# First product of seven experts by Strassen's block products, on one core

## The chip, the cores and the metric

The kernel runs on one core of a Trainium2 chip. A core has a matrix engine (TensorE, in the profile PE, with its weight loads as PEld), three engines for elementwise work (VectorE or DVE, ScalarE or ACT, GpSimd or POOL), a synchronisation engine (SP) and DMA queues. Each engine works through its own queue of instructions in order. Matmuls write into PSUM, which has eight banks of 128 x 512 f32; DVE and ACT read them there, GpSimd works on SBUF alone. The metric is the device time of one launch in microseconds. Before the change it was 794.83 us, the median of three runs (791.57 to 795.60).

## The reference, cut to what matters

Two stages follow each other: an attention over sorted blocks, whose output is `x` with N = 3072 rows and D = 512 columns, and a mixture of eight experts with F = 1024 hidden columns.

```python
logits = x @ w_gate
P = np.exp(logits - logits.max())
for _ in range(8):                       # the gate
    P /= P.sum(1, keepdims=True) + 1e-09
    P /= P.sum(0, keepdims=True) + 1e-09
    P *= N / E
out = np.zeros((N, D))
for e in range(E):
    h = np.maximum(x @ w1[e], 0.0)       # first product
    out += P[:, e:e + 1] * (h @ w2[e])   # second product
```

The gate needs the logits of all rows, so it can begin only when the attention of all four batches is done.

## The kernel before, in words

The program is written with a tile framework that gives buffers and semaphores and fixes, when the program is built, the order in which each engine's queue holds its instructions. That order can differ from the order of the source lines; on the chip it doesn't change any more.

**Attention.** Four batches of 768 rows. Their output lands transposed in `xtT` (128 partitions x 4 blocks of D x 3072 rows, bf16), and `logits` (L241) writes `glog`. While batch `bb` is in the attention, expert 0 is computed for batch `bb - 1` (`expert0`, L302): the two generators take turns on TensorE. Expert 0 for the last batch is left for after the attention.

**Gate.** L340 to L381. An identity `I128`, which `make_identity` writes on GpSimd, is used by the first matmul (L358) to find the greatest logit; then eight rounds of four DVE operations, one matmul for the column sums (L377) and three DVE operations. Meanwhile TensorE works on expert 0's last batch (L383) and on expert 1. Then 24 DVE scalings (L386) multiply expert 0's part of the sum `osbl` (f32, all 3072 rows) by its gate.

**Experts 1 to 7.** For each expert, six chunks of 512 rows go through `expert` (L280). A chunk's first half is eight blocks of 128 hidden columns: four matmuls of 128 x 128 by 128 x 512 over D into one bank (L285), then a relu on ACT into `hTs` (L287). Its second half is four blocks of 128 rows: eight matmuls over the hidden columns into one bank (L292), then DVE adds the bank times the gate to `osbl` (L395). A chunk has 64 matmuls, an expert 384. For the last expert each finished block of rows goes out by DMA (L399).

**Weights.** `load_expert` (L77) loads `w1e` and `w2e` of one expert, 1 MB each in SBUF, from f32 in HBM; the DMAs are issued from GpSimd's queue. There are buffers for four experts, in the pools `wp` and `wp2`, and expert e + 2 is loaded when expert e begins.

Of the kernel before, what the change touches and what calls it, by code (L numbers as in the profile page):

```python
# [24 lines left out]
def kernel(  # L25
# [23 lines left out]
    mps = ctx.enter_context(tc.tile_pool(name="mps", bufs=2))  # L49
    actx = ExitStack()  # L50
    kvp = actx.enter_context(tc.tile_pool(name="kvp", bufs=2))
    perp = actx.enter_context(tc.tile_pool(name="perp", bufs=1))
    vsp = actx.enter_context(tc.tile_pool(name="vsp", bufs=1))
# [11 lines left out]
    def load_batch(bb, n):  # L65
        for d, name in ((vt, "vt"), (kt, "kt"), (qt, "qt")):
            d[bb] = kvp.tile([128, 8, 384], BF16, name=name, bufs=1 if d is vt else 2)
        for l0 in range(0, 8, n):
            for d, src in ((vt, v), (kt, k), (qt, q)):
                nc.gpsimd.dma_start(  # L70
                    out=d[bb][:, l0:l0 + n, :],
                    in_=src[bb, l0:l0 + n].rearrange("h (p kk) d -> p h (kk d)", kk=6))

    w1t = {}
    w2t = {}

    def load_expert(e, pool):  # L77
        w1t[e] = pool.tile([128, 4, F], BF16, name="w1e")
        w2t[e] = pool.tile([128, 8, Dm], BF16, name="w2e")
        nc.gpsimd.dma_start(out=w1t[e], in_=moe_w1[e].rearrange("(kk k) f -> k kk f", k=128))  # L80
        nc.gpsimd.dma_start(out=w2t[e], in_=moe_w2[e].rearrange("(fb k) f -> k fb f", k=128))

    Ibig = ones.tile([128, 128], BF16)
# [4 lines left out]
    load_expert(0, wp)  # L88
    load_batch(1, 4)


# [33 lines left out]
    xtT = xtp.tile([128, 4, N], BF16)  # L125
# [36 lines left out]
    def queries(bb, hp, bank, first):  # L162

        qps = bank([128, 6, 128], BF16)
        if first:
            for h in range(2):
                for kk in range(6):
                    nc.tensor.matmul(qps[64 * h:64 * h + 64, kk, :],  # L168
                                     qt[bb][:, 2 * hp + h, kk * 64:kk * 64 + 64],
                                     Ibig, is_transpose=True, start=True, stop=True)  # L170
        else:
            qr = sp.tile([128, 6, 2, 64], BF16, name="qr")
            nc.gpsimd.tensor_copy(  # L173
                qr.rearrange("p kk h d -> p h kk d"),
                qt[bb][:, 2 * hp:2 * hp + 2].rearrange("p h (kk d) -> p h kk d", d=64))
# [74 lines left out]
    def attention(bb, bank, first=False):  # L250
        if first:
            for hp in range(4):
                queries(bb, hp, bank, True)
            for l0 in (0, 4):
                yield from sort_values(bb, l0, 4, bank)
        else:
            yield from sort_values(bb, 0, 8, bank)
        for s in range(7):
            if s < 4:
                if not first:  # L260
                    queries(bb, s, bank, False)
# [18 lines left out]
    def expert(e, c0, n, hp, op, done):  # L280
        hTs = mps.tile([128, 8, 512], BF16, name="hTs")
        for fb in range(8):
            hps = hp.tile([128, 512], F32, name="hps")
            for kk in range(4):
                nc.tensor.matmul(hps[:, 0:n], w1t[e][:, kk, fb * 128:(fb + 1) * 128],  # L285
                                 xtT[:, kk, c0:c0 + n], start=(kk == 0), stop=(kk == 3))
            nc.scalar.activation(out=hTs[:, fb, 0:n], in_=hps[:, 0:n], func=AF.Relu)  # L287
            yield
        for tt in range(n // 128):
            oacc = op.tile([128, Dm], F32, name="oacc")  # L290
            for fb in range(8):
                nc.tensor.matmul(oacc, hTs[:, fb, tt * 128:(tt + 1) * 128],  # L292
                                 w2t[e][:, fb, :], start=(fb == 0), stop=(fb == 7))
# [5 lines left out]
    def keep(t, oacc):  # L299
        nc.vector.tensor_copy(osbl[:, t, :], oacc)  # L300

    def expert0(bb, hp, op):  # L302
        for c in range(2):
            yield from expert(0, bb * S + c * 384, 384, hp, op, keep)
# [15 lines left out]
    with ExitStack() as c2:  # L320
        pa = c2.enter_context(tc.tile_pool(name="pa", bufs=4, space=bass.MemoryType.PSUM,
                                           reuse_waits="tile"))
        hp1 = c2.enter_context(tc.tile_pool(name="hp1", bufs=2, space=bass.MemoryType.PSUM,
                                            reuse_waits="tile"))
        op1 = c2.enter_context(tc.tile_pool(name="op1", bufs=2, space=bass.MemoryType.PSUM,
                                            reuse_waits="tile"))
        bank1 = lambda shape, dt: pa.tile(shape, dt, name="bank", tag="bank")
        for bb in range(1, B):
            build_r(bb, nc.gpsimd, 4)
            if bb + 1 < B:  # L330
                load_batch(bb + 1, 8)
            else:
                load_expert(1, wp)
            work = [attention(bb, bank1), expert0(bb - 1, hp1, op1)]
            while work:
                work = [w for w in work if next(w, 0) is None]
    actx.close()


    wp2 = ctx.enter_context(tc.tile_pool(name="wp2", bufs=2))  # L340
    mpc = ctx.enter_context(tc.tile_pool(name="mpc", bufs=1))
    gp = ctx.enter_context(tc.tile_pool(name="gp", bufs=2, space=bass.MemoryType.PSUM,
                                        reuse_waits="tile"))
    hp = ctx.enter_context(tc.tile_pool(name="hp", bufs=3, space=bass.MemoryType.PSUM,
                                        reuse_waits="tile"))
    op = ctx.enter_context(tc.tile_pool(name="op", bufs=3, space=bass.MemoryType.PSUM,
                                        reuse_waits="tile"))
    load_expert(2, wp2)

    onesc = mpc.tile([128, 128], F32)  # L350
    nc.vector.memset(onesc, 1.0)
# [31 lines left out]
    for _ in expert0(B - 1, hp, op):  # L383
        pass
    for t in range(NT):
        nc.vector.tensor_scalar(out=osbl[:, t, :], in0=osbl[:, t, :],  # L386
                                scalar1=glog[:, t, 0:1], scalar2=None, op0=ALU.mult)


    for e in range(1, E):  # L390
        if e + 2 < E:
            load_expert(e + 2, wp2 if (e + 2) % 4 in (2, 3) else wp)

        def add(t, oacc):
            nc.vector.scalar_tensor_tensor(  # L395
                out=osbl[:, t, :], in0=oacc, scalar=glog[:, t, e:e + 1],
                in1=osbl[:, t, :], op0=ALU.mult, op1=ALU.add)
# [36 lines left out]
```

## Time and profile before

| what | value |
|---|---|
| median of three runs | 794.83 us |
| span of the profiled execution, first to last instruction | 792.7 us |
| TensorE busy | 748.6 us, 94% of the span |
| DVE, ACT, GpSimd busy | 235.4, 287.6, 45.4 us |
| mean granted TensorE clock | 0.970 |
| one whole expert, 302.8 to 385.7 us | 82.9 us |
| data moved by DMA | 39.45 MB |

The profile is of one execution. Its own time is known as the span; the launch's time holds a little more than the span. A row of the groups or of the timeline names the line of the kernel, the engine, the operation, the tile written and the tile read, the shapes and a count. The figure in brackets behind a row of the timeline is how long the engine stood idle before it, and what released it. Busy time of TensorE is modelled at the ends of matmuls, so stretches of many matmuls say more than the duration of one.

### The profile page before, as it was taken

To read this page: it belongs to the slowest core of one execution; us is meant where nothing else is said; L and a number is where in the kernel's file an instruction comes from. 1 tells how busy PE (TensorE), PEld (TensorE's weight loads), DVE (VectorE), ACT (ScalarE), POOL (GpSimd) and SP (SyncE) were. 2 spreads that over 40 slices of the span, in tenths; PEclk is the share of its full clock that TensorE was granted. 3 is DMA by queue.
4 is the path that set the end of the run, shared out by engine and by line. 5 is a ranking of instruction groups with operands and counts; after the bars stand their busy time and mean duration, and the time that the engine had idled before them with its cause. 6 is when DMAs were issued, how large, how long until landed. Compare 5 with 4: busy or idle time off the path is not lost.

```text
span 792.7 us, 10003 instructions
## 1 busy us (share of the span) xinstructions
PE 748.6 (94%) x4244; PEld 368.0 (46%) x4244; DVE 235.4 (30%) x502; ACT 287.6 (36%) x524; POOL 45.4 (6%) x61
## 2 busy tenths in 40 slices
PE   2497989999999999999999999999999999999997
PEld 1374646565444444444444444444444444444443
DVE  4233524464871212212121222212121221212122
ACT  3353454543224243332424233342423333242432
POOL 3341110001000000000000000000000000000000
PEclk9658998999999999999999999999999999999999
DMA  9998250209800051003300240000000000002212
GB/s 163 224 212 173 41 120 2 81 2 186 132 1 1 1 82 25 1 0 56 52 1 0 33 74 0 1 1 1 0 1 1 1 0 1 1 0 80 80 67 93
DMA packets 33836, 39.45 MB, mean 50 GB/s; under 512 B 1664, under 2 KB 25984, under 8 KB 33792
## 3 DMA queue, kind: packets, MB, share of 16 engines
q0 software_dynamic: 25648, 26.22, 21.0%
q1 hardware_dynamic: 8144, 12.59, 4.8%
q8 instruction: 33, 0.54, 0.3%
q14 instruction: 11, 0.09, 0.0%
HBM read 55.60 MB, written 9.44 MB: 82 GB/s over the span
## 4 chain that ended last, share of the span: by engine, by line
PE 86%; DMA 7%; DVE 4%; ACT 1%; issue 1%; POOL 1%; POOLq 0%; ACTq 0%
PE hps L285 40%; PE oacc L292 40%; DMA vd<-vs 3%; DMA vsb<-vd 3%; PE bank L222 2%; DMA qt<-in_q_dram 1%; PE bank L206 1%; DVE osbl L386 1%; PE bank L236 1%; ACT vs L149 1%; PE bank L190 1%; PE bank L147 0%; PE bank L177 0%; PE gps L377 0%; PE bank L246 0%
## 5 line engine op out<-in xcount | busy, mean ns | idle before, releaser
L287 ACT ACTIVATE hTs<-hps 128x512 bf16<-128x512 f32 (+1 forms) x400 | 232.8, 583 | 414.4 <-PE hps L285 414.3
L285 PE MATMUL hps<-xtT,w1e 128*128 128x512 bf16 (+1 forms) x1600 | 354.1, 375 | 0.0
L292 PE MATMUL oacc<-w2e,hTs 128*128 128x512 bf16 x1536 | 345.8, 379 | 0.4 <-DVE osbl L395 0.4
L395 DVE SCALAR_TENSOR_TENSOR osbl<-oacc,glog,osbl 128x512 f32<-128x512 f32 x168 | 125.9, 750 | 437.4 <-PE oacc L292 437.4
L285 PEld LDWEIGHTS <-w1e 128*128 128x128 bf16 x1600 | 156.1, 99 | 173.3 <-issue 4.6
L292 PEld LDWEIGHTS <-hTs 128*128 128x128 bf16 x1536 | 147.8, 98 | 173.3 <-issue 0.9
L212 ACT ACTIVATE atp<-bank 96x384 bf16<-96x384 f32 x64 | 27.7, 483 | 44.4 <-PE bank L222 29.8
L222 PE MATMUL bank<-vsb,atp 96*96 96x128 bf16 x256 | 23.8, 255 | 19.2 <-DMA vsb<-vd 19.2
L222 PEld LDWEIGHTS <-atp 96*96 96x96 bf16 x256 | 22.1, 152 | 24.1 <-DMA vsb<-vd 20.5
L195 DVE CAST kTs<-bank 128x384 bf16<-128x384 f32 x32 | 16.8, 578 | 33.4 <-PE bank L190 33.4
L229 DVE TENSOR_TENSOR og<-bank,recips 96x256 bf16<-96x256 f32 x64 | 24.2, 410 | 0.4
L300 DVE COPY osbl<-oacc 128x512 f32<-128x512 f32 x24 | 16.5, 688 | 21.9 <-PE oacc L292 21.5
L80 POOL DMA_DIRECT2D w1e<-in_moe_w_dram x8 | 6.2, 771 | 277.5 <-PE hps L285 246.7
L228 DVE RECIPROCAL recips<-bank 96x4 f32<-96x4 f32 x64 | 9.9, 170 | 37.3 <-PE bank L222 37.0
L206 PEld LDWEIGHTS <-kTs 64*96 64x96 bf16 x256 | 14.5, 130 | 10.3 <-issue 6.4
L149 ACT CAST vs<-bank 128x384 bf16<-128x384 f32 x32 | 13.8, 507 | 14.7 <-PE bank L147 12.6
L206 PE MATMUL bank<-qTs,kTs 64*96 64x96 bf16 x256 | 18.3, 219 | 0.3 <-ACT atp L212 0.2
L180 ACT COPY qTs<-bank 128x768 bf16<-128x768 bf16 x16 | 12.9, 818 | 5.8 <-PE bank L168 4.0
L173 POOL COPY qr<-qt 128x768 bf16<-128x768 bf16 x12 | 9.9, 833 | 58.6 <-PE bank L177 55.7
L312 PE MATMUL bank<-Ibig,Prep 32*128 32x32 bf16 x8 | 0.5, 188 | 12.7 <-DVE Prep L123 12.7
L236 PE MATMUL bank<-Ibig,og 96*128 96x96 bf16 x128 | 10.1, 225 | 1.2 <-DVE og L229 1.2
L236 PEld LDWEIGHTS <-og 96*128 96x128 bf16 x128 | 7.8, 108 | 4.1 <-DVE og L229 2.8
(65 smaller groups left out, 146.1 us busy)
## 6 DMA issues: line engine op xcount, KB each, us to landing
w1e<-in_moe_w_dram POOLq DMA_DIRECT2D x8, 1024.0 KB, 8.1
w2e<-in_moe_w_dram POOLq DMA_DIRECT2D x8, 1024.0 KB, 10.9
out_dram<-osbl SPq DMA_DIRECT2D x24, 256.0 KB, 2.0
vd<-vs SPq DMA_DIRECT2D x3, 768.0 KB, 9.2
vsb<-vd SPq DMA_DIRECT2D x3, 768.0 KB, 5.7
vt<-in_v_dram POOLq DMA_DIRECT2D x4, 384.0 KB, 9.0
kt<-in_k_dram POOLq DMA_DIRECT2D x4, 384.0 KB, 10.3
qt<-in_q_dram POOLq DMA_DIRECT2D x4, 384.0 KB, 12.0
```

Source lines behind the costliest of these rows:

```text
L149: nc.scalar.copy(vs[:, :, h, :], vps.rearrange("p (kk d) -> p kk d", d=64))
L195: nc.vector.tensor_copy(kT[bb, hp][:, :, :, 3 * b:3 * b + 3], kps.rearrange("p kk (i c) -> p i c kk", i=8))
L206: nc.tensor.matmul(sps[0:96, j, :], kT[bb, hp][r, i].rearrange("p c kk -> p (c kk)"), qT[bb, hp][r, 16 * i:16 * i + 16].rearrange("p c kk ...
L212: nc.scalar.activation(out=at[bb, hp, h, b][0:96], in_=sps[0:96], func=AF.Exp, scale=scale)
L222: nc.tensor.matmul(ops[0:96, j].rearrange("p a d -> p (a d)"), at[bb, hp, h, b][0:96, j, :], mkap(vsbt[bb % 2], [[VW, 96], [NB * 512 - a, ...
L229: nc.vector.tensor_mul(og[bb, hp][0:96, 4 * b:4 * b + 4, h, :], ops[0:96, :, 0, :], mkap(recips, [[recips.ap[0][0], 96], [1, 4], [0, 64]]))
L236: nc.tensor.matmul(xps[:, i, :], og[bb, hp][0:96, i].rearrange("p h d -> p (h d)"), Ibig[0:96, 0:96], is_transpose=True, start=True, stop= ...
L285: nc.tensor.matmul(hps[:, 0:n], w1t[e][:, kk, fb * 128:(fb + 1) * 128], xtT[:, kk, c0:c0 + n], start=(kk == 0), stop=(kk == 3))
L287: nc.scalar.activation(out=hTs[:, fb, 0:n], in_=hps[:, 0:n], func=AF.Relu)
L292: nc.tensor.matmul(oacc, hTs[:, fb, tt * 128:(tt + 1) * 128], w2t[e][:, fb, :], start=(fb == 0), stop=(fb == 7))
L300: nc.vector.tensor_copy(osbl[:, t, :], oacc)
L395: nc.vector.scalar_tensor_tensor(out=osbl[:, t, :], in0=oacc, scalar=glog[:, t, e:e + 1], in1=osbl[:, t, :], op0=ALU.mult, op1=ALU.add)
```

## The change

For experts 1 to 7 the first product is put together by a scheme of Strassen's with seven block products in place of eight. Rows are taken in three blocks of 1024. In a block, D is cut into two halves, the hidden columns into two halves of 512, and the rows into two halves of 512. So `w1` has the blocks a11, a21 (first half of D; first and second half of the hidden columns), a12, a22 (second half of D), `x` has b11, b12 (first half of D; first and second 512 rows), b21, b22, and the hidden part has c11, c12, c21, c22. A step of `hidden` computes 128 columns of each half for all 1024 rows. It forms seven products of two matmuls each in four banks:

- y = a11 (b12 - b22), kept in s3, then + (a11 + a12) b22, which gives c12;
- z = (a21 + a22) b11, kept in s2, then + a22 (b21 - b11), which gives c21;
- v = (a11 + a22)(b11 + b22), kept in s1, then + (a12 - a22)(b21 + b22);
- w = (a21 - a11)(b11 + b12);
- GpSimd makes s3 = s3 - s2 and s1 = s1 + s3; then c22 = w + s1, and c11 = v + (z + s3 - y), on DVE.

All four results go through a relu into `hT` (two buffers of 128 x 8 x 1024, bf16): c12 and c21 on ACT, c11 and c22 by a custom DVE instruction that adds two operands and clips the sum from below at 0. s1, s2, s3 and t are single f32 buffers.

The sums of blocks are made once and kept in bf16: `xc` (five of `x` for each of the three blocks of rows; block 0 on DVE, blocks 1 and 2 on GpSimd) ahead of the gate, and `wc` (ten instructions per expert, on GpSimd; two buffers). Expert 1's are ahead of the gate too, those of expert e + 1 are written into the loop over expert e.

The second product of a block of 1024 rows, `output`, runs while the next block's `hidden` runs; the two generators take turns, in steps. In block 0 of expert 1 there is no earlier block, and behind block 2 of expert 7 there is `output` alone. PSUM is used as six banks for `hidden` and two for `output`. The pool `wp2` goes: there are buffers for two experts, and expert e + 1 is loaded during expert e, `w1` at its beginning and `w2` behind its first block of rows.

```diff
-    def load_expert(e, pool):
-        w1t[e] = pool.tile([128, 4, F], BF16, name="w1e")
-        w2t[e] = pool.tile([128, 8, Dm], BF16, name="w2e")
+    def load_w1(e):
+        w1t[e] = wp.tile([128, 4, F], BF16, name="w1e")
         nc.gpsimd.dma_start(out=w1t[e], in_=moe_w1[e].rearrange("(kk k) f -> k kk f", k=128))
+
+    def load_w2(e):
+        w2t[e] = wp.tile([128, 8, Dm], BF16, name="w2e")
         nc.gpsimd.dma_start(out=w2t[e], in_=moe_w2[e].rearrange("(fb k) f -> k fb f", k=128))
...
-    wp2 = ctx.enter_context(tc.tile_pool(name="wp2", bufs=2))
     mpc = ctx.enter_context(tc.tile_pool(name="mpc", bufs=1))
+    xcp = ctx.enter_context(tc.tile_pool(name="xcp", bufs=1))
+    wcp = ctx.enter_context(tc.tile_pool(name="wcp", bufs=2))
+    htp = ctx.enter_context(tc.tile_pool(name="htp", bufs=2))
+    fsp = ctx.enter_context(tc.tile_pool(name="fsp", bufs=1))
...
-    load_expert(2, wp2)
+    xc = xcp.tile([128, 5, 2, N // 2], BF16)
+    wct = {}
+
+    def sum_x(p, eng):
+        ta, tb = (slice(1024 * p + 512 * i, 1024 * p + 512 * i + 512) for i in range(2))
+        b11, b12, b21, b22 = (xtT[:, k:k + 2, t] for k in (0, 2) for t in (ta, tb))
+        for j, (a, b, o) in enumerate(((b11, b22, ALU.add), (b12, b22, ALU.subtract),
+                                       (b21, b11, ALU.subtract), (b11, b12, ALU.add),
+                                       (b21, b22, ALU.add))):
+            eng.tensor_tensor(out=xc[:, j, :, 512 * p:512 * p + 512], in0=a, in1=b, op=o)
+
+    def sum_w(e):
+        wct[e] = wcp.tile([128, 5, 2, F // 2], BF16, name="wc")
+        for kk in range(2):
+            a11, a21 = (w1t[e][:, kk, f:f + 512] for f in (0, 512))
+            a12, a22 = (w1t[e][:, 2 + kk, f:f + 512] for f in (0, 512))
+            for j, (a, b, o) in enumerate(((a11, a22, ALU.add), (a21, a22, ALU.add),
+                                           (a11, a12, ALU.add), (a21, a11, ALU.subtract),
+                                           (a12, a22, ALU.subtract))):
+                nc.gpsimd.tensor_tensor(out=wct[e][:, j, kk, :], in0=a, in1=b, op=o)
+                yield
+
+    sum_x(0, nc.vector)
+    for _ in sum_w(1):
+        pass
+    sum_x(1, nc.gpsimd)
+    sum_x(2, nc.gpsimd)
 
     onesc = mpc.tile([128, 128], F32)
     nc.vector.memset(onesc, 1.0)
     I128 = mpc.tile([128, 128], F32)
     make_identity(nc, I128)
...
-    for e in range(1, E):
-        if e + 2 < E:
-            load_expert(e + 2, wp2 if (e + 2) % 4 in (2, 3) else wp)
...
-        for c in range(6):
-            for _ in expert(e, c * 512, 512, hp, op, add):
-                pass
...
+    bk = ctx.enter_context(tc.tile_pool(name="bk", bufs=6, space=bass.MemoryType.PSUM,
+                                        reuse_waits="tile"))
+    op = ctx.enter_context(tc.tile_pool(name="op2", bufs=2, space=bass.MemoryType.PSUM,
+                                        reuse_waits="tile"))
...
+    def hidden(e, p, i, hT):
...
+        def add(ps, wa, xa, first):
+            for kk in range(2):
+                nc.tensor.matmul(ps, wa[:, kk, :], xa[:, kk, :],
+                                 start=(first and kk == 0), stop=(kk == 1),
+                                 skip_group_check=True)
...
+        y = bank()
+        add(y, a11, xc[:, 1, :, xs], True)
+        s3 = wide("s3")
+        nc.scalar.copy(s3, y)
+        z = bank()
+        add(z, wc[:, 1, :, fs], b11, True)
+        s2 = wide("s2")
+        nc.scalar.copy(s2, z)
+        nc.gpsimd.tensor_tensor(out=s3, in0=s3, in1=s2, op=ALU.subtract)
+        yield
+        v = bank()
+        add(v, wc[:, 0, :, fs], xc[:, 0, :, xs], True)
+        s1 = wide("s1")
+        nc.scalar.copy(s1, v)
+        nc.gpsimd.tensor_tensor(out=s1, in0=s1, in1=s3, op=ALU.add)
+        add(y, wc[:, 2, :, fs], b22, False)
+        nc.scalar.activation(out=c12, in_=y, func=AF.Relu)
+        yield
+        w = bank()
+        add(w, wc[:, 3, :, fs], xc[:, 3, :, xs], True)
+        add(z, a22, xc[:, 2, :, xs], False)
+        nc.scalar.activation(out=c21, in_=z, func=AF.Relu)
+        nc.vector._custom_dve(TENSOR_ADD_SAT, out=c22, in0=w, in1=s1, s0=TOP, s1=0.0)
+        t = wide("t")
+        nc.vector.tensor_tensor(out=t, in0=z, in1=s3, op=ALU.add)
+        yield
+        add(v, wc[:, 4, :, fs], xc[:, 4, :, xs], False)
+        nc.vector.tensor_tensor(out=t, in0=t, in1=y, op=ALU.subtract)
+        nc.vector._custom_dve(TENSOR_ADD_SAT, out=c11, in0=v, in1=t, s0=TOP, s1=0.0)
+        yield
+
+    def output(e, p, i, hT):
+        for j in range(2):
+            tt = 4 * j + i
+            t = 8 * p + tt
+            oacc = op.tile([128, Dm], F32, name="oacc")
+            for fb in range(8):
+                nc.tensor.matmul(oacc, hT[:, fb, tt * 128:(tt + 1) * 128],
+                                 w2t[e][:, fb, :], start=(fb == 0), stop=(fb == 7))
+                if fb == 3:
+                    yield
...
+    last = None
+    for e in range(1, E):
+        if e + 1 < E:
+            load_w1(e + 1)
+            sums = sum_w(e + 1)
+        else:
+            sums = iter(())
+        for p in range(3):
+            hT = htp.tile([128, 8, 1024], BF16, name="hT")
+            for i in range(4):
+                work = [hidden(e, p, i, hT)]
+                if last:
+                    work.append(output(*last[0:2], i, last[2]))
+                while work:
+                    work = [w for w in work if next(w, 0) is None]
+                if p or i > 1:
+                    next(sums, 0)
+            if p == 0 and e + 1 < E:
+                load_w2(e + 1)
+            last = (e, p, hT)
+    for i in range(4):
+        for _ in output(*last[0:2], i, last[2]):
+            pass
```

More of the change, by code (lines that the diff above doesn't have):

```diff
@@ L9 @@
 from concourse import bass_utils, mybir
+from concourse.dve_ops import TENSOR_ADD_SAT
 from concourse.masks import make_identity
@@ L48 @@
     xtp = ctx.enter_context(tc.tile_pool(name="xtp", bufs=1))
-    mps = ctx.enter_context(tc.tile_pool(name="mps", bufs=2))
     actx = ExitStack()
+    mps = actx.enter_context(tc.tile_pool(name="mps", bufs=2))
     kvp = actx.enter_context(tc.tile_pool(name="kvp", bufs=2))
@@ L87 @@
     nc.gpsimd.dma_start(out=wg, in_=moe_w_gate.rearrange("(kk k) e -> k kk e", k=128))
-    load_expert(0, wp)
+    load_w1(0)
+    load_w2(0)
     load_batch(1, 4)
@@ L277, in attention, with expert @@
         yield
-    def expert(e, c0, n, hp, op, done):
-        hTs = mps.tile([128, 8, 512], BF16, name="hTs")
+    def expert(e, c0, n, hsb, hp, op, done):
+        hTs = hsb()
         for fb in range(8):
@@ L300, in keep, with expert0 @@
         nc.vector.tensor_copy(osbl[:, t, :], oacc)
-    def expert0(bb, hp, op):
+    def expert0(bb, hsb, hp, op):
         for c in range(2):
-            yield from expert(0, bb * S + c * 384, 384, hp, op, keep)
+            yield from expert(0, bb * S + c * 384, 384, hsb, hp, op, keep)
     with tc.tile_pool(name="ps0", bufs=8, space=bass.MemoryType.PSUM,
@@ L332 @@
             else:
-                load_expert(1, wp)
-            work = [attention(bb, bank1), expert0(bb - 1, hp1, op1)]
+                load_w1(1)
+                load_w2(1)
+            work = [attention(bb, bank1),
+                    expert0(bb - 1, lambda: mps.tile([128, 8, 384], BF16, name="hTs"), hp1, op1)]
             while work:
@@ L337 @@
     actx.close()
-    wp2 = ctx.enter_context(tc.tile_pool(name="wp2", bufs=2))
     mpc = ctx.enter_context(tc.tile_pool(name="mpc", bufs=1))
[L342 to L347, printed above, removed]
@@ L348 @@
-    load_expert(2, wp2)
+    xcp = ctx.enter_context(tc.tile_pool(name="xcp", bufs=1))
+    wcp = ctx.enter_context(tc.tile_pool(name="wcp", bufs=2))
+    htp = ctx.enter_context(tc.tile_pool(name="htp", bufs=2))
+    fsp = ctx.enter_context(tc.tile_pool(name="fsp", bufs=1))
+    gctx = ExitStack()
+    gp = gctx.enter_context(tc.tile_pool(name="gp", bufs=2, space=bass.MemoryType.PSUM,
+                                         reuse_waits="tile"))
+    hp = gctx.enter_context(tc.tile_pool(name="hp", bufs=3, space=bass.MemoryType.PSUM,
+                                         reuse_waits="tile"))
@@ new lines @@
+    op = gctx.enter_context(tc.tile_pool(name="op", bufs=3, space=bass.MemoryType.PSUM,
+                                         reuse_waits="tile"))
+    xc = xcp.tile([128, 5, 2, N // 2], BF16)
[7 more added lines that the diff above has]
+            eng.tensor_tensor(out=xc[:, j, :, 512 * p:512 * p + 512], in0=a, in1=b, op=o)
@@ L381 @@
         nc.vector.tensor_mul(glog, glog, mkap(cs1, [cs1.ap[0], [0, NT], cs1.ap[1]]))
-    for _ in expert0(B - 1, hp, op):
+    for _ in expert0(B - 1, lambda: htp.tile([128, 8, 1024], BF16, name="hT"), hp, op):
         pass
@@ L387 @@
                                 scalar1=glog[:, t, 0:1], scalar2=None, op0=ALU.mult)
-    for e in range(1, E):
-        if e + 2 < E:
-            load_expert(e + 2, wp2 if (e + 2) % 4 in (2, 3) else wp)
-        def add(t, oacc):
+    gctx.close()
+    bk = ctx.enter_context(tc.tile_pool(name="bk", bufs=6, space=bass.MemoryType.PSUM,
+                                        reuse_waits="tile"))
+    op = ctx.enter_context(tc.tile_pool(name="op2", bufs=2, space=bass.MemoryType.PSUM,
+                                        reuse_waits="tile"))
@@ new lines, with bank, wide @@
+    TOP = 3.0e38
+    def hidden(e, p, i, hT):
+        ta, tb = (slice(1024 * p + 512 * j, 1024 * p + 512 * j + 512) for j in range(2))
+        fs = slice(128 * i, 128 * i + 128)
+        xs = slice(512 * p, 512 * p + 512)
+        def add(ps, wa, xa, first):
[3 more added lines that the diff above has]
+                                 skip_group_check=True)
+        def bank():
+            return bk.tile([128, 512], F32, name="bk")
+        def wide(name):
+            return fsp.tile([128, 512], F32, name=name)
+        wc, w1 = wct[e], w1t[e]
+        a11, a22 = w1[:, 0:2, fs], w1[:, 2:4, 512 + 128 * i:640 + 128 * i]
+        b11, b22 = xtT[:, 0:2, ta], xtT[:, 2:4, tb]
+        c11, c12 = hT[:, i, 0:512], hT[:, i, 512:1024]
+        c21, c22 = hT[:, 4 + i, 0:512], hT[:, 4 + i, 512:1024]
+        y = bank()
[28 more added lines that the diff above has]
+        yield
@@ L399, in add @@
                 nc.sync.dma_start(out=out[t * 128:(t + 1) * 128, :], in_=osbl[:, t, :])
-        for c in range(6):
-            for _ in expert(e, c * 512, 512, hp, op, add):
-                pass
+            yield
+    last = None
[21 more added lines that the diff above has]
+            pass
 _INS = ['q', 'k', 'v', 'sort_net', 'moe_w_gate', 'moe_w1', 'moe_w2']
```

## The prediction

> **What bounds the kernel now.** I read the page's shares first, then the groups by line, then the table by stages, then the timeline around the gate (the routing weights `glog`), because the change works on both sides of it.
>
> The page's busy times, and three of its costliest groups (line, engine, op, tile, count, then busy us and mean ns):
>
> ```profile
> PE 748.6 (94%) x4244; PEld 368.0 (46%) x4244; DVE 235.4 (30%) x502; ACT 287.6 (36%) x524; POOL 45.4 (6%) x61
> ...
> L287 ACT ACTIVATE hTs<-hps 128x512 bf16<-128x512 f32 (+1 forms) x400 | 232.8, 583 | 414.4 <-PE hps L285 414.3
> ...
> L395 DVE SCALAR_TENSOR_TENSOR osbl<-oacc,glog,osbl 128x512 f32<-128x512 f32 x168 | 125.9, 750 | 437.4 <-PE oacc L292 437.4
> ...
> w1e<-in_moe_w_dram POOLq DMA_DIRECT2D x8, 1024.0 KB, 8.1
> ```
>
> TensorE is busy 94% of the span, and ACT and DVE wait for it (the last columns). The table by stages (stretch, length, then PE, PEld, DVE, ACT, POOL busy us, granted clock, DMA):
>
> ```profile
> 177.00:179.80 2.80, 1.91 (x39) 1.49 (x40) 2.34 (x9) 0.00 (x0) 2.15 (x4) 0.89 0.20 11
> 179.80:182.40 2.60, 2.60 (x16) 1.25 (x14) 0.56 (x2) 0.49 (x1) 1.54 (x3) 0.50 1.07 181
> ...
> 302.80:385.70 82.90, 82.90 (x386) 37.55 (x384) 18.01 (x24) 28.66 (x48) 1.64 (x2) 1.00 0.16 26
> ```
>
> One expert is 384 matmuls in 82.90 us with TensorE never idle at full clock: 0.2159 us each. All other engines have room. The row at 179.8 shows what a thin stretch costs: after 2.8 us in which TensorE was busy 1.91, it ran 2.6 us at clock 0.50.
>
> GpSimd's own timeline, where the change puts most of its sums (start, us, engine, line):
>
> ```profile
> 26.30 2.12 POOL L135 TENSOR_TENSOR R<-Pb,mask 128x512 bf16<-128x512 f32 x2
> ...
> 102.18 0.94 POOL L70 DMA_DIRECT2D vt<-in_v_dram  x1 [16.60 <-PE bank L147]
> 103.12 0.84 POOL L173 COPY qr<-qt 128x768 bf16<-128x768 bf16 x1
> ...
> 180.18 0.33 POOL masks.py:199 TENSOR_SCALAR_AFFINE_SELECT I<-I 128x128 f32<-128x128 f32 x1
> ```
>
> A two-input elementwise of 512 columns takes GpSimd 1.04 us (2.12 and, elsewhere, 2.06 for two), a one-input copy of 768 takes 0.83. The identity I128, which the gate needs first, is ready at 180.5.
>
> TensorE's timeline at the gate:
>
> ```profile
> 174.71 1.03 PE L292 MATMUL oacc<-w2e,hTs 128*128 128x512 bf16 x4
> ...
> 186.38 0.81 PE L292 MATMUL oacc<-w2e,hTs 128*128 128x512 bf16 x3
> 187.12 0.38 PE L358 MATMUL gps<-I,gm 128*1 128x128 f32 x2
> ...
> 205.55 0.38 PE L285 MATMUL hps<-xtT,w1e 128*128 128x512 bf16 x1
> ...
> 215.34 0.39 PE L377 MATMUL gps<-cs,onesc 128*128 128x8 f32 x2 [0.35 <-DVE cs L375]
> ```
>
> The gate's chain runs from L358 at 187.12 to its eighth column sum, which ends at 215.73: 28.6 us. It is hidden: TensorE works on experts 0 and 1 between its steps and starts expert 1 at 205.55. Check of this reading: 205.55 + 2688 x 0.2159 + 1.8 for the five gate matmuls after it + 4.1 from the last matmul to the end = 791.8, against a span of 792.7. The median of the runs shown, 794.83, lies 2.1 above that span; I add 2.1 at the end.
>
> **What the change saves.** A step (an expert's 128 columns of each half, 1024 rows) has 14 hidden matmuls in place of 16. There are 7 x 3 x 4 = 84 steps: 168 x 0.2159 = 36.3 us less TensorE work. A step with its 16 output matmuls is 30 x 0.2159 = 6.48 us.
>
> **Engines in a step.** ACT: three copies and two relus, 5 x 0.60 (L287 at 128x512 is 597 ns) = 3.0. DVE: two L395 sums, two tensor_tensor, two custom adds; none of the last four is in the trace, I take 0.75 each for those with two wide inputs (L395) and 0.70 for the custom (between L300's 0.69 and 0.75): 4.4. GpSimd: two adds, 2.1. All are below 6.48, and the single buffers s1, s2, s3, t close a loop of about 3.4 us (ACT 0.60 twice, GpSimd 1.05, DVE 0.75, hand-overs 0.4). The tightest place is v of the next step, which takes the bank of y: y is read last by t - y, at about 6.6 us of its step, and v is wanted at 8.2. So the plain step stays bound by TensorE, with 1.6 us to spare. These edits cost nothing while that margin holds.
>
> **Where GpSimd's queue breaks it: the gate.** The scheduler fixes each queue's order in the built program. After the attention GpSimd's queue reads:
>
> ```
> xc sums x2, wc sums of expert 1 x10, xc sums x8, I128 memset, I128 select,
> w1 load of expert 2, wc sums of expert 2 x2, w2 load, wc sums x8, then the s3 and s1 adds of expert 1
> ```
>
> I128 stands behind 20 sums. The first waits for the last L292 of expert 0's third batch (175.74), so it starts near 176.0. The xc sums have 1024 columns, of which the trace has none: I take 2 x 1.04 = 2.08. So 10 x 2.08 + 10 x 1.04 = 31.2, with memset and select (0.23 and 0.33 and gaps, 0.9) I128 is ready at 208.1. TensorE, in order, gets to its first gate matmul after 32 hidden and 14 output matmuls, at 186.4 + 3.0 = 189.4, and stands for 18.7 us. Behind it is the rest of expert 0, about 13 us of work, which no longer covers the chain: the last four column sums follow each other with nothing between. By the chain's old length TensorE is free at 208.1 + 28.6 = 236.7 and DVE at 237.5.
>
> DVE then has the 24 scalings of `osbl` by `glog` (L386: 9.59 us) queued ahead of its first work for expert 1, which starts at 247.1. Block 0 of expert 1 has no output matmuls to hide this. Its four steps go by the loop of 3.4 us: the first z + s3 ends at 248.55, t - y of step 2 at 256.1, then v, its copy and v again bring TensorE to block 1 at 258.0. Left to TensorE alone it would have been 236.7 + 12.1 = 248.8. DVE's five xc sums cost nothing: the maximum of `glog` behind them is not wanted until 208.
>
> **Where it breaks it again: once per expert.** At the start of experts 2 to 6 the queue reads: w1 load of the next expert, s3 add of step 0, one wc sum, s1 add of step 0, nine wc sums, s3 add of step 1. Count from the expert's first matmul. The load waits for the last use of the old w1, in the third quarter of the step before (-2.15), goes out at -1.9 and lands 8.1 later, at 6.2; the wc sum waits for it. Behind it: s1 add of step 0 at 7.3 to 8.3 (wanted at 3.1), nine sums to 17.7, s3 and s1 adds of step 1 to 19.8. DVE's add of w and s1 waits, and behind it, in order, z + s3 and t - y. t - y of step 0 ends at 10.5: v of step 1 waits from 8.2 to 10.6. t - y of step 1 ends at 22.1: v of step 2 starts at 22.2, where it would have been 14.7. That is 7.5 us an expert, in waits of 2.4 and 5.1; five times, 37.5. Expert 7 has no sums to make.
>
> **Clock.** A wait of 5.1 us without a matmul has no like in this stage of the trace; the row at 179.8 puts 2.6 us at half clock behind a much thinner gap, 1.3 us lost. Bounds: nothing, and the same behind both waits (2.6 an expert). I take 1.3 for the long one: 6.5.
>
> [...]
>
> **Sum.** 258.0, + the rest of TensorE's work, (2520 - 56) x 0.2159 = 532.0, + 37.5 + 6.5 + 4.1 = 838.1 of span; + 2.1: 840 us.
>
> The unknown that matters is GpSimd's price. From below: the copy's rate, 0.83 / 768 x 512 = 0.56 per sum, which would mean that a second input is free. From above: the longest row of L135, 1.11. I take 1.04, the same operation. The new custom add has L229's form (410 ns at 256) below and no upper row; it would have to reach 1.5 before the margin of 1.6 goes. The landing has 7.8 below and 16.7 above (one early load beside many others); I take 8.1, as nothing else loads then.
>
> [...]
>
> **The rivals.**
> 1. GpSimd's adds on bf16 cost far less than L135's, and both waits shrink. At 0.56: I128 at 193.7, block 1 at 242.2, 1.2 an expert, no clock loss: 242.2 + 532.0 + 6.0 + 4.1 + 2.1 = 786, the only road I see to faster. It decides below about 0.6 per sum. Against it: six rows of L135 from 1.04 to 1.11. At 0.83 the same sum gives 818, still slower.
> 2. The waits per expert are covered (the load lands early and the adds overtake): 840 - 44 = 796, no change. Against it: the order is fixed, and nine sums alone are 9.4 us against a margin of 1.6. If only the load were instant, the loss is 4.4 an expert: 824.
> 3. DVE becomes the bound: a custom add of 2.5 makes 8.0 a step, 84 x 1.5 = 126 more before what it hides: some 920. Nothing in the trace speaks for so slow an add.
>
> **How the numbers follow.** Main case 0.84, rival 1 0.05, rival 2 0.05, rival 3 and the like 0.06. The range goes from GpSimd at 0.83 (818, less 4 without clock loss) to GpSimd at 1.11 (+6), the clock lost behind both waits (+6.5) and landings 2 us later, a quarter of the way to 16.7 (+10): 814 to 862. About 0.5% is what can be told from no change here: rival 1 gives faster 0.04 and part of same, rival 2 the rest of same, 0.04; slower 0.92.
>
> **What would show it.** Hidden matmuls number 1176 plus 256. GpSimd's first two-input sums at about 1.04 and 2.08 us; TensorE idle near 189 to 208 on GpSimd's I128; a second pause until about 237; 24 scalings on DVE ahead of the first custom add; at the start of experts 2 to 6 two pauses of TensorE of 2 to 3 and about 5 us, released by DVE, with DVE waiting for GpSimd and GpSimd for a DMA; plain steps of 6.5 us. Wrong if the sums take half, if the order counts for less because landings come earlier, or if plain steps are longer than 6.5.

## The result and the profile after

The changed kernel takes 869.26 us (median of 4 runs, 868.27 to 869.63) against 793.39 us for the kernel before (4 runs, 791.57 to 795.6): a ratio of 1.0963, 95% interval 1.0941 to 1.0985. The profiled execution has a span of 867.6 us. The forecast was 840, with a range of 814 to 862: the direction was right, the loss is 29 us larger than forecast, and the time lies above the range.

The page of the changed kernel, busy times and three groups (line, engine, op, tile, count, then busy us and mean ns, then idle time and its releaser), and the weight load:

```profile
PE 735.5 (85%) x4011; PEld 356.5 (41%) x4076; DVE 473.9 (55%) x843; ACT 318.2 (37%) x608; POOL 359.5 (41%) x309
...
L466 POOL TENSOR_TENSOR s<-s,s 128x512 f32<-128x512 f32 x84 | 106.4, 1266 | 290.6 <-ACT s L465 273.0
...
L480 DVE CUSTOM_DVE_ANT_0 hT<-bk,s 128x512 bf16<-128x512 f32 x84 | 58.1, 691 | 78.8 <-POOL s L472 69.8
...
w1e<-in_moe_w_dram POOLq DMA_DIRECT2D x8, 1024.0 KB, 8.3
```

TensorE has less to do and is busy a smaller share of a longer span. No engine is the bound: DVE is at 55%, the load lands in 8.3 us as before. The custom add costs 0.69 us, as forecast; GpSimd's f32 add costs 1.27 against the 1.04 that I took.

The waits of the changed kernel (engine, tile and line that waited, who released it: total us, times, longest):

```profile
DVE hT L480 <- POOL s L472: 69.8, 14, 8.3
PE bk L442 <- DVE hT L480: 35.0, 13, 5.6
...
PE gps L397 <- POOL I masks.py:199: 22.7, 1, 22.7
PE gps L416 <- DVE cs L414: 21.5, 7, 12.4
```

These are the two places of the forecast: TensorE at the gate (once for the identity, 22.7, and 21.5 for the column sums), and TensorE behind DVE behind GpSimd in the hidden products (35.0).

GpSimd's timeline (start, us, engine, line; in brackets the idle time ahead and what ended it):

```profile
174.33 4.19 POOL L370 TENSOR_TENSOR xc<-xtT 128x1024 bf16<-128x1024 bf16 x2 [29.47 <-PE bank L226]
178.49 13.37 POOL L380 TENSOR_TENSOR wc<-w1e 128x512 bf16<-128x512 bf16 x10
191.82 16.61 POOL L370 TENSOR_TENSOR xc<-xtT 128x1024 bf16<-128x1024 bf16 x8
...
208.65 0.29 POOL masks.py:199 TENSOR_SCALAR_AFFINE_SELECT I<-I 128x128 f32<-128x128 f32 x1
...
231.70 0.92 POOL L84 DMA_DIRECT2D w2e<-in_moe_w_dram  x1
232.65 8.89 POOL L380 TENSOR_TENSOR wc<-w1e 128x512 bf16<-128x512 bf16 x8
...
512.54 1.15 POOL L380 TENSOR_TENSOR wc<-w1e 128x512 bf16<-128x512 bf16 x1 [3.57 <-PE oacc L495]
513.64 1.26 POOL L472 TENSOR_TENSOR s<-s,s 128x512 f32<-128x512 f32 x1
514.87 10.03 POOL L380 TENSOR_TENSOR wc<-w1e 128x512 bf16<-128x512 bf16 x9
```

The identity stands behind twenty sums, and nine sums stand in one run at the start of expert 4, as the queue's order said. New to me is what the eight sums at 232.65 did to DVE. The timeline of TensorE and DVE at the gate, and then of TensorE in expert 4:

```profile
209.00 0.58 PE L397 MATMUL gps<-I,gm 128*1 128x128 f32 x2 [22.67 <-POOL I masks.py:199]
...
232.16 9.60 DVE L413 TENSOR_TENSOR glog<-glog,rs 128x192 f32<-128x192 f32 x1
...
249.03 0.60 PE L416 MATMUL gps<-cs,onesc 128*128 128x8 f32 x2 [2.75 <-DVE cs L414]
...
250.50 11.63 DVE L425 TENSOR_SCALAR osbl<-osbl,glog 128x512 f32<-128x512 f32 x24
262.05 0.68 DVE L480 CUSTOM_DVE_ANT_0 hT<-bk,s 128x512 bf16<-128x512 f32 x1
...
515.69 0.59 PE L442 MATMUL bk<-xc,wc 128*128 128x512 bf16 x2 [1.50 <-DVE hT L480]
516.98 1.01 PE L442 MATMUL bk<-xtT,wc 128*128 128x512 bf16 x2 [0.70 <-ACT s L461]
...
528.24 1.01 PE L442 MATMUL bk<-xc,wc 128*128 128x512 bf16 x2 [3.37 <-DVE hT L480]
529.52 1.01 PE L442 MATMUL bk<-xtT,wc 128*128 128x512 bf16 x2 [0.28 <-ACT s L461]
```

One small multiplication of the gate (L413, 0.36 us in the other iterations) lasted 9.60 us and ended with GpSimd's eighth sum (232.65 + 8.89 = 241.54). In expert 4 TensorE stands for 2.20 and 3.65 us. The table by stages of the changed kernel there (stretch, length, then PE, PEld, DVE, ACT, POOL busy us, granted clock, DMA):

```profile
514.10:516.90 2.80, 0.68 (x3) 0.19 (x2) 1.93 (x3) 0.56 (x2) 2.80 (x3) 1.00 0.00 0
516.90:520.30 3.40, 3.32 (x8) 1.13 (x8) 1.97 (x4) 1.60 (x4) 3.40 (x4) 0.51 0.00 0
...
524.70:528.20 3.50, 0.16 (x1) 0.00 (x0) 0.71 (x2) 0.00 (x0) 2.68 (x3) 0.86 0.00 0
528.20:533.40 5.20, 4.89 (x12) 1.61 (x12) 3.37 (x5) 2.16 (x4) 2.54 (x2) 0.50 0.02 3
533.40:536.00 2.60, 2.60 (x12) 1.09 (x11) 2.04 (x3) 0.60 (x1) 0.00 (x0) 0.87 0.01 3
```

Behind the two pauses the granted clock was 0.51 for 3.4 us and 0.50 for 5.2. Lost clock is 3.4 x 0.49 + 5.2 x 0.50 + 2.6 x 0.13 = 4.6 us, pauses 5.85, together 10.5. The loads of w1 follow each other at 88.5 us (327.12, 415.86, 504.12, 592.64, 681.28), against 12 x 6.475 = 77.7 for twelve undisturbed steps: 10.8 an expert.

### The profile page after: what moved, and what is told of

Its sections match the earlier page's. It is cut to its first block, busy times and chain, and to the rows that moved or that the text cites. A ratio compares the mean times of both kernels' runs of the same rounds, so it can differ in the third digit from the quotient of the medians.

```text
span 867.6 us, 10667 instructions
## 1 busy us (share of the span) xinstructions
PE 735.5 (85%) x4011; PEld 356.5 (41%) x4076; DVE 473.9 (55%) x843; ACT 318.2 (37%) x608; POOL 359.5 (41%) x309
## 4 chain that ended last, share of the span: by engine, by line
PE 63%; DMA 11%; POOL 11%; DVE 6%; ACT 3%; issue 3%; another core or an unknown queue 2%; POOLq 0%; ACTq 0%; DVEq 0%; SPq 0%
PE oacc L495 28%; PE bk L442 24%; POOL wc L380 5%; DMA w1e<-in_moe_w_dram 4%; DMA vd<-vs 4%; PE hps L289 3%; PE oacc L296 3%; DMA vsb<-vd 2%; POOL xc L370 2%; POOL s L472 2%; PE bank L226 2%; DVE glog L413 1%; POOL s L466 1%; DVE osbl L425 1%
## 5 line engine op out<-in xcount | busy, mean ns | idle before, releaser
L495 PE MATMUL oacc<-w2e,hT 128*128 128x512 bf16 x1326 | 347.6, 386 | 1.4 <-issue 0.2
L466 POOL TENSOR_TENSOR s<-s,s 128x512 f32<-128x512 f32 x84 | 106.4, 1266 | 290.6 <-ACT s L465 273.0
L495 PEld LDWEIGHTS <-hT 128*128 128x128 bf16 x1344 | 133.7, 100 | 166.8 <-issue 13.3
L442 PE MATMUL bk<-xc,wc 128*128 128x512 bf16 x488 | 154.4, 397 | 35.2 <-DVE hT L480 35.0
L442 PEld LDWEIGHTS <-wc 128*128 128x128 bf16 x840 | 84.1, 100 | 151.9 <-issue 60.7
L461 ACT COPY s<-bk 128x512 f32<-128x512 f32 x84 | 49.2, 585 | 249.4 <-PE bk L442 189.5
L442 PE MATMUL bk<-xtT,wc 128*128 128x512 bf16 x336 | 104.6, 394 | 6.9 <-ACT s L461 6.2
L472 POOL TENSOR_TENSOR s<-s,s 128x512 f32<-128x512 f32 x84 | 106.6, 1269 | 6.2
L480 DVE CUSTOM_DVE_ANT_0 hT<-bk,s 128x512 bf16<-128x512 f32 x84 | 58.1, 691 | 78.8 <-POOL s L472 69.8
L442 PE MATMUL bk<-xc,w1e 128*128 128x512 bf16 x319 | 99.7, 391 | 1.6 <-ACT s L465 0.7
L380 POOL TENSOR_TENSOR wc<-w1e 128x512 bf16<-128x512 bf16 x70 | 80.6, 1186 | 26.1 <-DMA w1e<-in_moe_w_dram 10.9
L479 ACT ACTIVATE hT<-bk 128x512 bf16<-128x512 f32 x84 | 50.2, 597 | 100.6 <-PE bk L442 100.5
L471 ACT COPY s<-bk 128x512 f32<-128x512 f32 x84 | 49.4, 588 | 42.0 <-PE bk L442 42.0
L442 PEld LDWEIGHTS <-w1e 128*128 128x128 bf16 x336 | 34.0, 101 | 43.4 <-issue 6.5
L474 ACT ACTIVATE hT<-bk 128x512 bf16<-128x512 f32 x84 | 50.7, 604 | 2.0 <-PE bk L442 1.1
L465 ACT COPY s<-bk 128x512 f32<-128x512 f32 x84 | 49.7, 592 | 1.8 <-PE bk L442 1.7
```

The lines of the kernel that those rows point to most:

```text
L380: nc.gpsimd.tensor_tensor(out=wct[e][:, j, kk, :], in0=a, in1=b, op=o)
L442: nc.tensor.matmul(ps, wa[:, kk, :], xa[:, kk, :], start=(first and kk == 0), stop=(kk == 1), skip_group_check=True)
L466: nc.gpsimd.tensor_tensor(out=s3, in0=s3, in1=s2, op=ALU.subtract)
L472: nc.gpsimd.tensor_tensor(out=s1, in0=s1, in1=s3, op=ALU.add)
L474: nc.scalar.activation(out=c12, in_=y, func=AF.Relu)
L480: nc.vector._custom_dve(TENSOR_ADD_SAT, out=c22, in0=w, in1=s1, s0=TOP, s1=0.0)
```

## The experiments

Two theories stood at the start. By the first, the extra loss comes mainly from the identity standing behind the sums: the gate's chain begins late, loses its cover and falls beside expert 2's sums. By the second, it comes from the sums themselves, wherever the identity is: they hold DVE's instructions beside them, as the multiplication that took 9.60 us in place of 0.36, and what is queued behind. The kernel before was run beside them, with medians of 793.2 us for the first four runs below and 792.3 for the last four; each ratio is against its own.

### The identity ahead of the sums

```
+    I128 = mpc.tile([128, 128], F32)
+    make_identity(nc, I128)
     sum_x(0, nc.vector)
     ...
     nc.vector.memset(onesc, 1.0)
-    I128 = mpc.tile([128, 128], F32)
-    make_identity(nc, I128)
```

> The identity I128 is written ahead of the 20 block sums on GpSimd; nothing else changes. Theory 1 (order alone: the engines do not hold each other): the gate's first matmul starts near 187 instead of 209, the eight rounds end near 217 to 220, the 24 scalings near 230, block 1 of expert 1 starts near 242 instead of 275: 835 us. Theory 2 (DVE instructions with two SBUF inputs are held while GpSimd works through back-to-back sums, as one multiplication of the gate was for 9.6 us): the gate's multiplications by row and column scalars are held until GpSimd's run ends near 208, and again by expert 2's sums; the gate ends near 243: 860 us or a little more. In between (each of the 16 multiplications held for one sum of 1 to 2 us): 845 to 850.

Measured: 853.88 us, ratio 1.0768 [1.0734, 1.0803]. That lies between the two theories, nearer to the second. The gate began 23.7 us earlier (185.32 in place of 209.00), and its eighth column sum came only 13.8 earlier (235.27 in place of 249.03). Groups of this kernel, DVE between 184 and 262:

```profile
L412 DVE TENSOR_SCALAR rs<-rs 128x24 f32<-128x24 f32 x8 | 15.1, 1884 | 0.3
...
L414 DVE TENSOR_TENSOR glog<-glog,rs 128x192 f32<-128x192 f32 x8 | 6.6, 819 | 0.2
```

the same two in the kernel before, with its 24 scalings:

```profile
L386 DVE TENSOR_SCALAR osbl<-osbl,glog 128x512 f32<-128x512 f32 x24 | 9.6, 481 | 0.0
...
L374 DVE TENSOR_TENSOR glog<-glog,rs 128x192 f32<-128x192 f32 x8 | 2.9, 358 | 0.3
...
L372 DVE TENSOR_SCALAR rs<-rs 128x24 f32<-128x24 f32 x8 | 1.5, 191 | 0.3
```

and the timeline of GpSimd and DVE with the identity first:

```profile
190.22 19.44 POOL L370 TENSOR_TENSOR xc<-xtT 128x1024 bf16<-128x1024 bf16 x9
193.10 1.59 DVE L412 TENSOR_SCALAR rs<-rs 128x24 f32<-128x24 f32 x1
195.49 1.46 DVE L414 TENSOR_TENSOR glog<-glog,rs 128x192 f32<-128x192 f32 x1
196.99 0.49 DVE L415 TENSOR_REDUCE cs<-glog 128x8 f32<-128x192 f32 x1
...
224.08 0.92 POOL L84 DMA_DIRECT2D w2e<-in_moe_w_dram  x1
224.77 9.18 DVE L412 TENSOR_SCALAR rs<-rs 128x24 f32<-128x24 f32 x1
225.03 8.89 POOL L380 TENSOR_TENSOR wc<-w1e 128x512 bf16<-128x512 bf16 x8
```

Adding a constant to 24 columns (L412) takes 0.19 us in the kernel before and here 1.88 on the mean, 0.84 without the longest; the multiplication (L414) takes 0.82 in place of 0.36. The lines at 193.10 and 195.49 show each of them held for most of one sum of GpSimd. The reduction (L415) that follows is not held: 0.49 here, 0.50 before. The addition asked for at 224.77, while GpSimd was busy with the issue of a load, was held for all eight sums that followed.

### Without the sums that stand beside the gate

Expert 2 uses expert 1's weight sums.

```
-            sums = sum_w(e + 1)
+            if e == 1:
+                wct[2] = wct[1]
+                sums = iter(())
+            else:
+                sums = sum_w(e + 1)
```

> The ten wc sums of expert 2, which stand beside the last rounds of the gate, are left out (expert 2 uses expert 1's sums, so its output is another); all other sums stay. Theory 1: nothing waits for these sums, 868 us as before. Theory 2: the multiplication that took 9.6 us takes 0.36, the gate ends 9 us earlier: 859 us. The pauses of TensorE at the start of experts 2 to 6 stay at about 10.8 us each in both.

Measured: 857.81 us, ratio 1.0818 [1.0782, 1.0853], 11.4 less than the changed kernel. L413 takes 0.36 us in every iteration and the scalings begin at 241.4 in place of 250.5. So the ten sums cost 9.1 us at the gate, although nothing waits for their results there. The rest of the 11.4 lies behind it: the loads of w1 follow each other at 88.0 us in place of 88.5, and why, no run shows.

### Without any sums in the loop

All experts use expert 1's weight sums.

```
-            sums = sum_w(e + 1)
+            wct[e + 1] = wct[1]
+            sums = iter(())
```

> No wc sums after expert 1's (all experts use expert 1's, so the output is another). If GpSimd's run of ten sums is what stops TensorE at the start of experts 2 to 6, with the half clock behind it, all five lose their 10.8 us: 54 us less than without expert 2's sums alone, 805 us. Rival (the w1 load, the single buffers or the banks are what stops it): pauses stay, 840 us or more. Plain steps 6.48 us.

Measured: 806.46 us, ratio 1.0170 [1.0136, 1.0204], 51.4 less than the run above: 10.3 for each of the five experts. The loads of w1 follow each other at 77.7 us (318.26, 395.96, 473.66), as twelve undisturbed steps do, and the mean granted clock of the profiled execution is 0.947 against 0.926 in that of the run above. The pauses and the half clock behind them come from these sums.

### The same sums, one in each step

Everything is computed; each sum is put behind the s1 add of its step. `mark` keeps that add, and `tc.issue_after` queues what is written under it behind it.

```
-        nc.gpsimd.tensor_tensor(out=s1, in0=s1, in1=s3, op=ALU.add)
+        mark.append(nc.gpsimd.tensor_tensor(out=s1, in0=s1, in1=s3, op=ALU.add))
...
-                    next(sums, 0)
+                    with tc.issue_after(mark[-1].ins):
+                        next(sums, 0)
```

> The wc sums of the next expert are queued on GpSimd behind the s1 add of their step, one a step from the third step on; everything is computed. Theory: GpSimd has 1.27 + 1.27 + 1.1 = 3.65 us of work in a step of 6.48 and nothing waits for it, so the pauses go as if the sums were left out, and expert 2's no longer stand beside the gate: 805 us (within 2 of the run without loop sums). Rival (one more sum in a step makes s3 or s1 late, or the load is late): pauses of about 1 us in most steps, 830 us or more. I128's place is unchanged, so TensorE still stands about 22 us at the gate.

Measured: 805.24 us, ratio 1.0155 [1.0122, 1.0188]: as fast as with no sums in the loop. So it was their place in the queue, not their work. GpSimd's timeline of this kernel, one step:

```profile
333.64 1.27 POOL L467 TENSOR_TENSOR s<-s,s 128x512 f32<-128x512 f32 x1 [3.86 <-ACT s L466]
334.99 1.27 POOL L473 TENSOR_TENSOR s<-s,s 128x512 f32<-128x512 f32 x1
336.22 1.16 POOL L380 TENSOR_TENSOR wc<-w1e 128x512 bf16<-128x512 bf16 x1
```

and one stretch of its table by stages (columns as above):

```profile
361.00:439.00 78.00, 78.00 (x363) 35.34 (x361) 49.10 (x72) 33.18 (x61) 43.56 (x37) 1.00 0.17 28
```

GpSimd needs 3.7 of a step's 6.48 us, and TensorE is never idle, at full clock.

### The gate's scalars in PSUM

The identity first, and the tiles that hold the row and the column scalars of the gate moved to a PSUM bank (taken from `op`).

```
+    gr = gp.tile([128, 128], F32, name="gr", bufs=1)
-    rs2 = mpc.tile([128, NT], F32)
+    rs2 = gr[:, 0:NT]
-    cs1 = mpc.tile([128, E], F32)
+    cs1 = gr[:, 64:64 + E]
```

> As the run with the identity first (853.9 us), but the row and column scalars of the gate lie in PSUM, so that none of its DVE instructions has more than one input in SBUF and none runs from SBUF to SBUF. Theory (a DVE instruction is held by GpSimd's sums only if it takes a second operand, or its second half, through SBUF): the gate's rounds run at their free pace of 3.2 to 3.4 us beside the sums, the gate ends near 214 to 217 instead of 236.7; the 24 scalings are then held by expert 2's ten sums instead, which end near 234; block 0 of expert 1 starts on DVE near 236 to 240 instead of 248.4: 844 us. Rival (DVE is held by GpSimd whatever its operands): no change, 854 us.

Measured: 844.80 us, ratio 1.0661 [1.0626, 1.0695], 9.1 less than with the identity first alone. Groups of this kernel, DVE between 184 and 262:

```profile
L427 DVE TENSOR_SCALAR osbl<-osbl,glog 128x512 f32<-128x512 f32 x24 | 23.1, 1038 | 0.0
...
L415 DVE TENSOR_TENSOR glog<-glog,gr 128x192 f32<-128x192 f32 x8 | 2.8, 352 | 0.2
...
L413 DVE TENSOR_SCALAR gr<-gr 128x24 f32<-128x24 f32 x8 | 1.5, 190 | 0.2
```

and its timeline of GpSimd and DVE inside the scalings:

```profile
218.12 12.37 DVE L427 TENSOR_SCALAR osbl<-osbl,glog 128x512 f32<-128x512 f32 x2
...
219.15 0.92 POOL L84 DMA_DIRECT2D w2e<-in_moe_w_dram  x1
220.09 8.89 POOL L380 TENSOR_TENSOR wc<-w1e 128x512 bf16<-128x512 bf16 x8
```

With the gate's scalars out of SBUF the same instructions are not held beside the sums of x: the multiplication takes 0.35 in all eight rounds, the addition 0.19, where it took 1.59 in three rounds with the identity first alone. Whether an instruction takes a second half through SBUF, as the expectation has it, no run shows. Here the rounds end before expert 2's sums begin (215.95 and 216.77), so the long hold of 9.18 is not put to the test. The column sums end 20.8 us earlier than with the identity first alone (214.47 begins the eighth, against 235.27). More than half of that is lost again: the 24 scalings, from SBUF to SBUF, now meet expert 2's sums and take 23.1 us in place of 11.6. Two of them lasted 12.37 us together. The second, which fills at least the last 10.4 of it (from 220.10), was also asked for while GpSimd issued the load of w2, and it ended only behind the eight sums and the f32 add that followed them without a gap (at 230.2).

### The load of w2 behind the sums

In the changed kernel GpSimd issues expert 2's w2 load between its second and its third sum, and DVE was held from that point for all eight. Here the load is issued behind the tenth.

```
-            if p == 0 and e + 1 < E:
+            if p == 0 and e + 1 < E and e > 1:
                 load_w2(e + 1)
+            if p == 2 and e == 1:
+                with tc.issue_after(mark[2].ins):
+                    load_w2(2)
```

> The changed kernel with the w2 load of expert 2, which stood between the second and the third of expert 2's ten sums, queued behind all ten. Theory (the multiplication was held through eight sums because it was asked for while the load was being issued): now each of the gate's instructions beside the sums is held for at most one sum of 1.1 us; about three rounds run beside them, three instructions each: the gate ends some 4 us earlier, 865 us. Rival (a run of sums is never broken once it has begun): one instruction is held for up to ten sums, 869 to 871 us.

Measured: 861.92 us, ratio 1.0877 [1.0840, 1.0914], 7.3 less than the changed kernel. Its timeline:

```profile
229.54 11.59 POOL L381 TENSOR_TENSOR wc<-w1e 128x512 bf16<-128x512 bf16 x10 [7.28 <-DMA w1e<-in_moe_w_dram]
230.83 1.19 DVE L421 TENSOR_TENSOR glog<-glog,cs 128x192 f32<-128x192 f32 x1
232.44 0.62 DVE L412 TENSOR_SCALAR rs<-rs 128x24 f32<-128x24 f32 x1
233.43 0.92 DVE L414 TENSOR_TENSOR glog<-glog,rs 128x192 f32<-128x192 f32 x1
```

The longest instruction of the gate in these rows, beside ten sums in one run, takes 1.19 us. The long holds stand in the three profiled executions (the changed kernel, the identity first, the scalars in PSUM) in which DVE asked while GpSimd was issuing a DMA ahead of a run of sums, and not in this one. Why the whole run of sums then goes first, no run shows. The scalings begin at 244.76 in place of 250.50: 5.7 of the 7.3 us lie at the gate.

### One sum a step and the identity first

Both edits together.

> Both repairs that need only another order: I128 ahead of the sums, and the wc sums one a step. The pauses per expert are gone (805 us with the gate as it was); at the gate, without expert 2's sums, the 9.2 us of one held instruction go too: the gate ends near 224 instead of 239 in the spread run: 790 us, about the kernel before (0.99 to 1.00). Rival (the gate's instructions, held one sum each by the first 20 sums, eat the whole gain): 800 us.

Measured: 793.12 us, ratio 1.0009 [0.9995, 1.0023]: the time of the kernel before. The eighth column sum begins at 228.32, against 239.06 with the sums spread alone, and 215.34 in the kernel before. Here 36.3 us less TensorE work is eaten by about as much loss at the gate and in the first block of expert 1.

### Nothing beside the gate

Expert 1's first product is the plain one, so no sum is wanted before expert 2. The fifteen sums of x and expert 2's weight sums are on GpSimd behind the last of the 24 scalings; experts 2 to 7 use seven products, with their sums one a step.

```
-    sum_x(0, nc.vector)
-    for _ in sum_w(1):
-        pass
-    sum_x(1, nc.gpsimd)
-    sum_x(2, nc.gpsimd)
     ...
+    gd = mpc.tile([128, 1], F32)
+    mark.append(nc.gpsimd.tensor_copy(gd, osbl[:, NT - 1, 0:1]))
+    with tc.issue_after(mark[-1].ins):
+        for p in range(3):
+            sum_x(p, nc.gpsimd)
     ...
-                work = [hidden(e, p, i, hT)]
+                work = [(hidden if e > 1 else plain)(e, p, i, hT)]
```

`plain` makes four column blocks of a step with four matmuls and a relu each, out of `bk`, and the pool `op2` is opened ahead of `bk`.

> Expert 1's first product by the plain eight block products, in the same steps; all 15 xc sums and expert 2's wc sums on GpSimd behind the last of the 24 scalings, beside expert 1; experts 2 to 7 by the seven products with the sums one a step. Theory: the gate is covered by experts 0 and 1 as before the change, no DVE instruction of the gate stands beside a sum, and of the saving six experts' 31.1 us remain, less 2 us at the first outputs and some 3 to 6 us in block 0 of expert 2 if it is not covered (here expert 1's last outputs cover it): 763 us, ratio 0.962. Rival (the seven products cost TensorE more than the plain step in some way not seen): above 775.

Measured: 761.96 us (760.49 to 763.62, 4 runs), ratio 0.9622 [0.9597, 0.9648]. It beats the kernel before, 792.31 us beside it, by 30.4 us (27.9 to 31.9 by the interval). Six experts with 24 matmuls less each are 6 x 24 x 0.2159 = 31.1. The page of this kernel and one stretch of its stages:

```profile
PE 715.2 (94%) x4100; PEld 352.5 (46%) x4100; DVE 422.3 (56%) x790; ACT 314.1 (41%) x596; POOL 326.7 (43%) x281
```

```profile
367.50:445.50 78.00, 78.00 (x364) 35.33 (x362) 49.08 (x72) 33.37 (x62) 43.55 (x37) 1.00 0.17 28
```

TensorE is at 94% again, and within the interval nothing of the saving is lost.

## Why the prediction was right and wrong

**What held.** The saving is real: the last experiment keeps 30.4 of the 31.1 us worked out for six experts. The plain step is 6.475 us (forecast 6.48), the margin of 1.6 held, and the custom adds (0.69) are no bound; rival 3 is out. Rivals 1 and 2 are out as well: the sums cost 2.11 us at 1024 columns (forecast 2.08) and 1.11 to 1.19 at 512 (1.04), and the nine sums of an expert are not covered. The identity is ready at 208.9 (208.1), after which the gate's first matmul starts at once. That this time is so near is partly luck: the sums began 1.7 us earlier than forecast (174.33) and took 34.1 us in place of 31.2. The larger part of the difference is DVE's five sums of x, which the sum put at nothing: the five wc sums beside them took 7.84 us, the next five 5.57. TensorE also came to the gate earlier (186.3, forecast 189.4) and so stood there for 22.7 us in place of 18.7; that does not move what follows. Both places of loss are where the order of GpSimd's queue put them.

**The step that failed first: "By the chain's old length TensorE is free at 208.1 + 28.6 = 236.7 and DVE at 237.5", then the scalings at 9.59.** From the gate's first matmul to the end of the eighth column sum it took 40.6 us. One multiplication lasted 9.60 in place of 0.36, held behind eight sums of expert 2. The other 2.8 are not due to expert 2's sums: without them the same stretch (209.03 to 240.53) is still 31.5 us in place of 28.6. Part of it is TensorE's pairs of small matmuls, which in the last three rounds took 0.60 in place of 0.38, at a granted clock of 0.50; the rest is not taken apart. The 24 scalings took 11.63, with two GpSimd adds of 1.3 among them. So DVE's first work for expert 1 starts at 262.05, not 247.1: 15.0 of the 29 us. The run without expert 2's sums takes 9.1 of it away, the run with the w2 load behind them 5.7.

The old length could not be used, because in the kernel before the chain ran beside a GpSimd that had no sums to make. The forecast put no price on what stands beside GpSimd's sums, neither on DVE's five sums of x nor on the gate. It was expert 2's sums, which the queue's order already placed beside the gate, that met the gate's own multiplications. With the identity first the multiplication took 0.82 us on the mean, both inputs in SBUF, and 0.35 with one of them in PSUM; the constant added to 24 columns took 1.59 beside the sums of x against 0.19, and the reduction was not held (0.49 against 0.50). Two of the holds here lasted eight sums (9.60 and 9.18 us) and a third eight sums and an f32 add (at least 10.4).

**The same place, smaller: "Its four steps go by the loop of 3.4 us".** A step of block 0 took 4.7 to 5.2 us, since two f32 adds of 1.27 and their hand-overs stand in the loop; from DVE's first work to block 1 it was 13.2 in place of 10.9 (2.2 us), and block 1's first step took 8.3 in place of 6.5 (1.8). The gate is 15.0 + 2.2 + 1.8 = 19.0 us over the forecast.

**The second step that failed, in size: "I take 1.3 for the long one: 6.5".** The pauses were shorter than forecast (5.85 an expert in place of 7.5): v took the bank that the first custom add (L480) frees, a DVE instruction earlier than the t - y that I had put there. The clock was the larger term: half clock followed both pauses and cost 4.6 an expert in place of 1.3. By the pitch of the loads an expert loses 10.8 in place of 8.8, five times 2.0 is 10. My own upper bound, half clock behind both waits, was 2.6 an expert, taken from one stretch of 2.6 us; the halving lasted 3.4 and 5.2. It followed idle pieces of 1.50 and 0.70 us as it did those of 3.37 and 0.28; how short a pause brings it, no run shows.

19 and 10 make the 29 us between the forecast span of 838.1 and 867.6. The upper end of the range, 862, took in dearer sums, lost clock and late landings, but no price for what the gate's instructions pay beside the sums. Either excess alone would have stayed inside the range (859 and 850 us); the two together do not.

## What to carry to other kernels

Work that was put on an engine with time to spare was not free here, where other work stood behind it in that engine's queue (10.3 us an expert) and where another engine's instructions beside it were held (9.60 us for a multiplication of 0.36). So read the built order of the queue, name the first instruction behind each run of added work, and then list what the other engines do at that time and where their operands lie: with one input in PSUM the gate's multiplication took 0.35 us, with both in SBUF 0.82 on the mean. A chain that was measured beside an idle engine has to be priced again when that engine is busy (28.6 us before, 40.6 in the changed kernel). Spread such work one piece a step: the same fifty sums cost 51 us in runs of nine and nothing one at a time.

## What the runs showed of the hardware that I had not expected

- A DVE instruction from SBUF to SBUF on 24 columns took 9.18 us, and a multiplication of 192 columns 9.60, both asked for while GpSimd was issuing a DMA with eight sums behind it, and a scaling of 512 columns at least 10.4 in the same place; beside ten sums in one run and no DMA among them the longest instruction of the gate in the rows shown took 1.19.
- Held: the f32 multiplications with both inputs in SBUF (0.82 us on the mean, 0.36 before), the constant added to 24 columns (1.59 in three rounds, 0.19 before), the scalings of 512 columns from SBUF to SBUF (24 in 23.1 us beside sums, 9.59 without). Not held: the reduction (0.49, 0.50 before), the reciprocal (0.30 beside sums and before), and the gate's multiplications and additions with the scalars in PSUM (0.35 and 0.19).
- GpSimd is held as well: five bf16 sums of 512 columns took 7.84 us beside DVE's sums of x, and the next five, without them, 5.57.
- The custom adds, which read one operand from PSUM, keep 0.69 us beside GpSimd's sums (the one at 514.94 in the changed kernel; 0.68 to 0.69 in all 84 of L480).
- In expert 4 of the changed kernel two idle pieces of 1.50 and 0.70 us close together were followed by half clock (0.51) for 3.4 us, 3.4 and 0.3 us by half clock (0.50) for 5.2.
- GpSimd's f32 add of 512 columns takes 1.27 us, its bf16 sums of 512 columns 1.11 (8.89 for eight in a run) to 1.19 (the mean of all 70), of 1024 columns 2.11.
